# Attention and mixture kernel on Trainium2: reciprocals of all batches spread by TensorE, loads moved to slot 10 without their wait for transposes, attends at every second slot

## The chip, the cores and the metric

The kernel runs on one core of one Trainium2 chip. The metric is the time of one execution in device microseconds. Executions of one kernel mostly agreed within about 0.35%, so effects of half a per cent need several runs and a comparison on the same chip. All runs quoted here are fast (none was more than 1.5% above the fastest of its kernel).

TensorE appears in the profile as PE (matmuls) and PEld (weight loads), VectorE as DVE, ScalarE as ACT, GpSimd as POOL. SP is SyncE; its work here is to issue DMAs, and SPq is its queue.

## The reference, cut to what matters

```python
def _attn_ref(q, k, v):                      # 8 batches, 8 heads, 576 tokens, head size 64
    ...                                      # phi(x): relu(x) times cos and sin weights, 128 features
    kv  = einsum('bhsf,bhsd->bhfd', phi(k), v)
    z   = sum(phi(k), axis=2)
    num = einsum('bhsf,bhfd->bhsd', phi(q), kv)
    den = einsum('bhsf,bhf->bhs', phi(q), z)[..., None] + 1e-06
    return num / den

def _moe_ref(x, w_gate, w1, w2):             # x: 4608 tokens x 512; 8 experts, inner size 1024
    P = exp(x @ w_gate - max)                # then 8 rounds of row and column normalisation
    for e in range(8):
        out += P[:, e:e+1] * (relu(x @ w1[e]) @ w2[e])
```

## The kernel before: the parts that matter

The first fifth of the run interleaves two things on TensorE: the feed-forward of expert 0, in blocks of 512 tokens, and the attention of the batches to come. A block `j` has 16 slots; each slot is four or so 512-wide matmuls of expert 0, followed by the pieces of attention work listed for that slot. In block `j`, the batch `b = j + 1` gets its denominators and its attends, batch `b + 1` is prepared (relu, weights, transposition of q), and batch `b + 2` is loaded. The trace shows ACT taking its instructions in the order in which they are written: it stood for 6.31 us, until 110.99 us, before a k tile that was not loaded yet, while PE waited (5.08 us, until 112.21) for ACT's next instruction. The text reads the other engines in the same way, which is an assumption.

```python
def load(b, half, names="qkv", held_back=False):        # issued on POOL
    for name in names:
        x = ld.tile([P, 2, C, D], F16, name=f"{name}_ld")
        ...
        i = nc.gpsimd.dma_start(out=..., in_=...)
        if held_back:
            after(ve.last, i)        # wait for the last DVE operation written so far
            after(turned[0], i)      # wait for the last transpose written so far

def prep_q(b, hk):                   # four times per batch; q_p has 3 buffers
    ...                              # DVE: relu, then q_p = q * weights
    turned[0] = nc.sync.dma_start(out=qTs[b, hk], in_=q_p..., transpose=True)   # on SP

def denominators(b):
    ...                              # PE: 24 matmuls of zsel with qTs[b, 0..3], written h by h
    ve.reciprocal(out=den[:], in_=den[:])
    if b >= 3:                       # spread over the 64 features of a head by DMA
        r = dram.tile([96, C3 * HP], FP32, name="r")
        nc.sync.dma_start(out=r[:], in_=den[:])
        for hk in range(HK):
            for hh in range(2):      # 8 reads that repeat a row over 64 partitions
                nc.sync.dma_start(out=rb[hh * HP : (hh + 1) * HP, :]..., in_=r[:]...)
        return
    ...                              # b < 3: hi and hl = den as two fp16 parts (DVE)

def attend(b, hk):
    if not by_dma:                   # b < 3: 3 matmuls with a 0/1 matrix spread hl over features
        te.matmul(out=rb_ps[i]..., lhsT=spread..., rhs=hls[b][:])
        se.copy(out=rb[...], in_=rb_ps[i]...)          # ACT, 384 and 192 wide
    ...                              # PE: num_ps = kv x qT;  DVE: xT = num_ps * rb
```

Names that come up in the profiles: `zsel` holds the sums of k, and the zsel matmuls with transposed q make the denominators; `kv_sb` is k times v, copied out of PSUM by ACT; `hT` is the hidden layer of expert 0 after its relu, copied out of `h_ps` by ACT; `xT` is what attention hands to the experts.

The two `rb_ps`, the two `num_ps`, the sums and the denominators all come from one pool of four PSUM banks (`small_ps`). The schedule, for blocks 2 to 6 (`at(block, slot, ...)`):

```python
at(j, 5 if j <= 2 else 4, denominators, b)
at(j, 8 + 2 * hk if j == 1 else 12 + hk, attend, b, hk)          # hk = 0..3
prep_q of batch b+1 at slots 5, 7, 8, 9; prep_kv at 6, 8, 10, 12; prep_k at 4, 6, 9, 11
at(j, 10, sums, b + 1, 0)
at(j, 13 + 2 * half, load, b + 2, half, "qkv", True)             # blocks 1 to 5
```

Block 1 prepares later than the others: its four `prep_q` of batch 3 stand at slots 7, 10 and 13 and at slot 0 of block 2.

Of the kernel before, what the change touches and what calls it, by code (L numbers as in the profile page):

```python
# [10 lines left out]
FP32 = mybir.dt.float32  # L11
# [14 lines left out]
def kernel(  # L26
# [10 lines left out]
    nc = tc.nc  # L37
    P = nc.NUM_PARTITIONS
# [4 lines left out]
    HP = P // 2  # L43
# [137 lines left out]
    with ExitStack() as p1:  # L181
# [10 lines left out]


        loaded = {}
        turned = [None]
        sources = {"q": q, "k": k, "v": v}

        def load(b, half, names="qkv", held_back=False):
            for name in names:
                x = ld.tile([P, 2, C, D], F16, name=f"{name}_ld")  # L200
                view = sources[name][b].rearrange("(hk hh) (p c) d -> (hh p) hk (c d)", hh=2, c=C)
                i = nc.gpsimd.dma_start(
                    out=x[:].rearrange("p hk c d -> p hk (c d)"),
                    in_=view[:, 2 * half : 2 * half + 2],
                )
                if held_back:

                    after(ve.last, i)
                    after(turned[0], i)
                for i in range(2):  # L210
                    loaded[name, b, 2 * half + i] = x[:, i]

# [88 lines left out]
        ve.tensor_copy(out=wg[:], in_=wg_ld[:])  # L301


        kps, qps, qTs, kvs, hls, rbs = {}, {}, {}, {}, {}, {}

        lent = acc_lo[:, G_LO - 4 : G_LO, :].rearrange("p g d -> p (g d)").bitcast(F16)
        VA = C * (D + 2)
# [18 lines left out]
        def prep_q(b, hk):  # L326

            q16 = loaded.pop(("q", b, hk))
            by_dma = b >= 2
            if by_dma:  # L330
                ve.tensor_scalar(
                    out=q16, in0=q16, scalar1=0.0, scalar2=None, op0=ALU.max
                )
            q_p = qp_pool.tile([P, C, 2, D], F16, name="q_p")
            ve.tensor_tensor(
                out=q_p[:], in0=q16.unsqueeze(2).to_broadcast([P, C, 2, D]),
                in1=cs, op=ALU.mult,
            )
            if by_dma:
                qTs[b, hk] = q_pTs[(b * HK + hk) % len(q_pTs)]  # L340
                turned[0] = nc.sync.dma_start(
                    out=qTs[b, hk], in_=q_p[:].rearrange("p c a d -> p (c a d)"),
                    transpose=True,
                )
            else:
                qps[b, hk] = q_p
# [72 lines left out]
        def denominators(b):  # L419

            zsel = kvs[b][1]
            den_ps = ps_s.tile([P, 512], FP32, name="small_ps")
            for h in range(H):
                hk, hh = h // 2, h % 2
                for j in range(3):
                    te.matmul(
                        out=den_ps[32 * j : 32 * j + 32, 0 : C3 * HP],
                        lhsT=zsel[:, h, :],
                        rhs=qTs[b, hk][:, j * C3 : (j + 1) * C3, hh * HP : (hh + 1) * HP],
                        start=(h == 0),  # L430
                        stop=(h == H - 1),
                    )
            den = kv_pool.tile([96, C3 * HP], FP32, name="den")
            ve.tensor_scalar(
                out=den[:], in0=den_ps[0:96, 0 : C3 * HP], scalar1=1e-6 / XS, scalar2=None,
                op0=ALU.add,
            )
            ve.reciprocal(out=den[:], in_=den[:])
            if b >= 3:

                r = dram.tile([96, C3 * HP], FP32, name="r")
                nc.sync.dma_start(out=r[:], in_=den[:])
                for hk in range(HK):
                    rb = rb_pool.tile([P, C * HP], FP32, name="rb")
                    for hh in range(2):
                        h = 2 * hk + hh
                        nc.sync.dma_start(  # L447
                            out=rb[hh * HP : (hh + 1) * HP, :].rearrange(
                                "p (j s) -> p j s", j=3
                            ),  # L450
                            in_=r[:].rearrange("(j r) s -> r j s", r=32)[h : h + 1].to_broadcast(
                                [HP, 3, C3 * HP]
                            ),
                        )
                    rbs[b, hk] = rb
                return

            hi = kv_pool.tile([96, C3 * HP], F16, name="hi")
            ve.tensor_copy(out=hi[:], in_=den[:])
            hl = kv_pool.tile([96, C3 * HP], F16, name="hl")  # L460
            ve.scalar_tensor_tensor(
                out=hl[:], in0=hi[:], scalar=lo[0:96], in1=den[:], op0=ALU.mult, op1=ALU.add
            )
            hls[b] = hl

        def attend(b, hk):

            parts = ((0, 2 * C3), (2 * C3, C))
            rb = rbs.pop((b, hk), None)
            rb_ps = [ps_s.tile([P, 512], FP32, name="small_ps") for _ in parts if rb is None]  # L470
            by_dma = rb is not None
            if not by_dma:
                rb = rb_pool.tile([P, C * HP], FP32, name="rb")
            for i, (c0, c1) in enumerate(parts):
                if by_dma:
                    break
                for j in range(c0 // C3, c1 // C3):
                    te.matmul(
                        out=rb_ps[i][:, (j * C3 - c0) * HP : ((j + 1) * C3 - c0) * HP],
                        lhsT=spread[0:96, j, hk].rearrange("p hh d -> p (hh d)"),  # L480
                        rhs=hls[b][:],
                        start=True,
                        stop=True,
                    )
                se.copy(out=rb[:, c0 * HP : c1 * HP], in_=rb_ps[i][:, 0 : (c1 - c0) * HP])
            num_ps = [ps_s.tile([P, 512], FP32, name="small_ps") for _ in parts]
            for i, (c0, c1) in enumerate(parts):
                for hh in range(2):
                    te.matmul(
                        out=num_ps[i][hh * HP : (hh + 1) * HP, 0 : (c1 - c0) * HP],  # L490
                        lhsT=kvs[b][0][:, hk, hh, :],
                        rhs=qTs[b, hk][:, c0:c1, hh * HP : (hh + 1) * HP],
                        start=True,
                        stop=True,
                    )
                ve.tensor_tensor(
                    out=xT[:, hk, b * S + c0 * HP : b * S + c1 * HP],
                    in0=num_ps[i][:, 0 : (c1 - c0) * HP],
                    in1=rb[:, c0 * HP : c1 * HP],
                    op=ALU.mult,  # L500
                )
# [89 lines left out]
        for j in range(B):  # L591
            b = j + 1
            if j == 0:

                at(0, 4, lambda: begun.append(sums_begun(1, 0)))
                at(0, 5, lambda: sums_made(1, 0, begun[2]))
                at(0, 6, lambda: begun.append(sums_begun(1, 1)))
                at(0, 7, prep_q, 1, 0)
                at(0, 7, prep_q, 1, 1)
                for hk in range(HK):  # L600
                    for i in range(3):
                        at(0, 7 + hk, turn, 1, hk, i)
                    if hk == 0:
                        at(0, 7, lambda: sums_made(1, 1, begun[3]))
                    if hk < 2:
                        at(0, 7 + hk, prep_q, 1, hk + 2)
                at(0, 10, denominators, 1)
                at(0, 11, gates, 0)
                for hk in range(HK):
                    at(0, min(13 + hk, 15), attend, 1, hk)  # L610
            elif b < B:
                if j <= 2:
                    at(j, 0, prep_q, b, 3)
                    at(j, 1, prep_kv, b, 3)
                    at(j, 1, sums, b, 0)
                    at(j, 3, sums, b, 1)
                    for i, (hk, k_) in enumerate(turns[2:]):
                        at(j, i // 2, turn, b, hk, k_, k_ != 1)
                else:
                    at(j, 0, sums, b, 1)  # L620
                    for i, (hk, k_) in enumerate(turns[8:]):
                        at(j, i, turn, b, hk, k_, k_ != 1)
                at(j, 5 if j <= 2 else 4, denominators, b)
                for hk in range(HK):
                    at(j, 8 + 2 * hk if j == 1 else 12 + hk, attend, b, hk)
            if j:
                at(j, 6, gates, j)
            if j <= 1:
# [15 lines left out]
                at(j, 10, sums, b + 1, 0)  # L644
            if 1 <= j and b + 2 < B:
                for half in range(2):
                    at(j, 13 + 2 * half, load, b + 2, half, "qkv", True)
        y_pss = {}
        for j in range(B - 1):
            if j:  # L650
# [521 lines left out]
```

## Time and profile before

| | before |
|---|---|
| time, median of the runs taken beside the change | 1014.13 us |
| PE busy | 972.6 us of a span of 1010.5 |
| blocks 2 to 6, from the timeline of PE | 24.7, 26.7, 24.6, 24.8, 18.5 us |
| PE waits for ACT in those blocks | 14.6 us, 4 times |

The page of the profiled execution opens with busy time by engine. Its second part cuts the span into 40 slices of 25 us, with the busy share and the granted TensorE clock in tenths. Its fourth part is the chain of work that ended last, followed back from the end of the run: how much of the span was spent on whom.

```profile
PE 972.6 (96%) x7786; PEld 675.3 (67%) x7786; DVE 808.5 (80%) x1828; ACT 552.5 (55%) x1220; POOL 60.3 (6%) x82
...
PEclk8999899999999999999999999999999999999999
DMA  9949999563100431134002331043013410104535
...
PE 83%; DMA 9%; DVE 3%; ACT 1%; issue 1%; SPq 1%; POOL 1%; POOLq 0%; DVEq 0%; ACTq 0%
```

PE looks full. But the chain holds 9% of DMA, and the slices with a busy DMA are the first eight, about 200 us. That is where the change works. From about 195 us on nothing differs between the two kernels.

The next view is the list of waits between 50 and 200 us: who waited for whom, microseconds in total, times, longest.

```profile
POOL q_ld L202 <- DMA q_pT<-q_p: 43.2, 2, 22.2
...
POOL q_ld L202 <- DMA acc_hi<-q_p: 21.3, 1, 21.3
...
ACT k_ld L109 <- DMA k_ld<-in_k_dram: 19.4, 4, 6.3
...
PE h_ps L109 <- ACT hT L109: 14.6, 4, 5.1
```

Read upwards, these lines are one chain. PE waits for a PSUM buffer that ACT has not emptied (hT, 14.6 us). ACT has not, because it stands before a k tile whose load is late (19.4 us). POOL issued that load late, because it waited for transposes (43.2 and 21.3 us; q_pT, acc_lo and acc_hi are all places where transposed q is kept). The timeline of SP's queue in block 3 shows why the transposes were late. Columns: start, duration, instruction, count.

```profile
106.62 0.33 SPq L442 DMA_DIRECT2D r<-den  x1
109.09 2.38 SPq L341 DMA_TRANSPOSE q_pT<-q_p  x1
113.37 6.20 SPq L447 DMA_DIRECT2D rb<-r  x8
119.83 3.09 SPq L341 DMA_TRANSPOSE q_pT<-q_p  x1
123.03 2.38 SPq L341 DMA_TRANSPOSE acc_lo<-q_p  x1
125.52 1.30 SPq L341 DMA_TRANSPOSE acc_hi<-q_p  x1
```

The eight rb reads wait for the r write to land (6.68 us after its issue, at 113.30) and then take 6.2 us of issue. Three transposes stand behind them. The next load waits for the last transpose, issued at 125.52, and was issued at 129.38. The following block's k tile is then late again: a ring. The load and ACT's wait for its k tile, from the timelines of POOL and ACT:

```profile
129.38 0.72 POOL L202 DMA_DIRECT2D q_ld<-in_q_dram  x1 [21.29 <-DMA acc_hi<-q_p]
```

```profile
135.69 0.68 ACT L109 ACTIVATE k_ld<-k_ld 128x576 f16<-128x576 f16 x1 [4.32 <-DMA k_ld<-in_k_dram]
```

The loads of block 1 were issued at 77.30, before there was any rb read (the first at 88.60); the last that POOL had waited for was DVE (acc_lo).

The timeline of PE shows what a gap costs (blocks 2 and 3; the bracket is the idle time before the group and what ended it).

```profile
80.51 0.51 PE L109 MATMUL small_ps<-q_pT,zsel 128*32 128x192 f16 x12
...
85.53 1.04 PE L109 MATMUL h_ps<-xT,w1e 128*128 128x512 f16 x4 [2.83 <-ACT hT L109]
86.39 4.44 PE L109 MATMUL y_ps<-w2e,hT 128*128 128x512 f16 x12
...
112.21 1.87 PE L109 MATMUL h_ps<-xT,w1e 128*128 128x512 f16 x4 [5.08 <-ACT hT L109]
```

Four 512-wide matmuls take 1.04 us at a granted clock of 1.00 (85.5 to 86.4 us) and 1.87 after the gap of 5.08 us, at 0.50 (110.3 to 117.1 us). The twelve behind the first gap take 4.44 us; the clock was 0.50 there from 86.4 to 89.8 us. So each of these gaps was paid for twice: once as idle time, once as matmuls at half clock behind it.

### The profile page before, as it was taken

The page shows a single profiled execution, that of the slowest core. Times are in us where ns is not written, and L with a number is a line of the kernel's source. Part 1 is how long each engine was busy: PE and PEld are TensorE (multiplying, and loading weights), DVE is VectorE, ACT ScalarE, POOL GpSimd, SP SyncE. Part 2 cuts the span into 40 slices and gives each one's busy share as a digit, 9 for nine tenths or more (in the row PEclk, how much of TensorE's full clock was granted, in tenths as well). Part 3 has the DMA queues.
Part 4 walks back from the last instruction along what each step waited for, and adds up shares of the span by engine and source line. Part 5 has one row for each costly group of instructions (what it writes and reads, how often), then busy time and mean ns, then how long its engine had stood idle before and what let it go on. Part 6 is the DMA issues. An engine that isn't in the chain of part 4 may idle for free.

```text
span 1010.5 us, 20082 instructions
## 1 busy us (share of the span) xinstructions
PE 972.6 (96%) x7786; PEld 675.3 (67%) x7786; DVE 808.5 (80%) x1828; ACT 552.5 (55%) x1220; POOL 60.3 (6%) x82
## 2 busy tenths in 40 slices
PE   7998788998999999999999999999999999999997
PEld 6444333445777777777777777777777777777775
DVE  5876555488898888898889888889789888988886
ACT  5764343446777655555555555555555555555551
POOL 6301111001000000000000000000000000000001
PEclk8999899999999999999999999999999999999999
DMA  9949999563100431134002331043013410104535
GB/s 167 204 76 176 156 173 172 103 129 66 38 34 24 90 66 33 40 66 87 27 25 58 61 70 38 25 89 66 24 49 66 78 36 25 48 25 104 135 85 126
DMA packets 89216, 79.81 MB, mean 79 GB/s; under 512 B 33984, under 2 KB 81056, under 8 KB 89120
## 3 DMA queue, kind: packets, MB, share of 16 engines
q1 hardware_dynamic: 61648, 47.33, 20.2%
q0 software_dynamic: 27232, 30.94, 19.6%
q8 instruction: 61, 1.00, 0.4%
q10 hardware_dynamic: 240, 0.26, 0.1%
q14 instruction: 35, 0.29, 0.1%
HBM read 89.01 MB, written 13.34 MB: 101 GB/s over the span
## 4 chain that ended last, share of the span: by engine, by line
PE 83%; DMA 9%; DVE 3%; ACT 1%; issue 1%; SPq 1%; POOL 1%; POOLq 0%; DVEq 0%; ACTq 0%
PE rows_ps L109 33%; PE h_ps L109 25%; PE copied_ps L109 11%; PE p_ps L109 11%; DMA rb<-r 2%; DMA q_pT<-q_p 2%; PE small_ps L109 2%; PE y_ps L109 2%; DMA k_ld<-in_k_dram 1%; DMA v_ld<-in_v_dram 1%; DMA q_ld<-in_q_dram 1%; SPq L447 1%; DMA r<-den 1%; DVE xT L109 1%; DVE den L109 1%
## 5 line engine op out<-in xcount | busy, mean ns | idle before, releaser
L845 DVE SCALAR_TENSOR_TENSOR acc_lo<-rows_ps,P_tok,acc_lo 128x512 f32<-128x512 f32 (+1 forms) x322 | 203.5, 641 | 74.8 <-PE rows_ps L109 74.8
L109 PEld LDWEIGHTS <-H 128*128 128x128 f16 x2080 | 203.0, 98 | 83.1 <-issue 1.2
L109 PEld LDWEIGHTS <-w1e 128*128 128x128 f16 x1632 | 156.7, 98 | 82.9 <-issue 23.2
L781 ACT CAST u<-h_ps 128x384 f16<-128x384 f32 x288 | 137.8, 478 | 131.2 <-PE h_ps L109 131.2
L775 DVE CUSTOM_DVE_ANT_0 H<-p_ps,u 128x384 f16<-128x384 f32 x329 | 181.4, 551 | 6.6 <-PE p_ps L109 6.5
L109 PEld LDWEIGHTS <-hs 128*128 128x128 f16 x1500 | 146.5, 98 | 56.4 <-issue 0.3
L109 PE MATMUL h_ps<-xT,w1e 128*128 128x384 f16 (+1 forms) x616 | 152.5, 354 | 17.8 <-ACT hT L109 14.6
L109 PE MATMUL h_ps<-S,w1e 128*128 128x384 f16 x672 | 164.1, 326 | 1.1 <-ACT u L109 0.9
L109 PE MATMUL p_ps<-xT,T 128*128 128x384 f16 x672 | 164.1, 326 | 0.1
L109 PE MATMUL rows_ps<-V,H 128*128 128x256 f16 x1000 | 150.0, 273 | 0.7 <-DVE acc_hi L845 0.7
L109 PE MATMUL rows_ps<-w2e,hs 128*128 128x256 f16 x1000 | 150.0, 273 | 0.0
L813 ACT ACTIVATE H<-h_ps 128x384 f16<-128x384 f32 x144 | 70.7, 491 | 95.0 <-PE h_ps L109 95.0
L109 PEld LDWEIGHTS <-T 128*128 128x128 f16 x1008 | 98.1, 98 | 29.5 <-issue 3.2
L109 PE MATMUL rows_ps<-w2e,H 128*128 128x256 f16 (+1 forms) x568 | 91.2, 285 | 0.0
L794 ACT COPY copied_ps<-h_ps 128x384 f32<-128x384 f32 x144 | 67.5, 468 | 35.4 <-PE h_ps L109 35.4
L109 PE MATMUL h_ps<-S,T 128*128 128x384 f16 x336 | 81.8, 325 | 0.4 <-ACT copied_ps L109 0.3
L109 PE MATMUL copied_ps<-xT,w1e 128*128 128x384 f16 x336 | 82.1, 326 | 0.0
L804 ACT ACTIVATE H<-copied_ps 128x384 f16<-128x384 f32 x144 | 70.9, 492 | 20.3 <-PE copied_ps L109 20.3
L109 PE MATMUL copied_ps<-w2e,H 128*128 128x256 f16 x504 | 75.5, 272 | 0.0
L109 PE MATMUL rows_ps<-V,hs 128*128 128x256 f16 x500 | 75.0, 272 | 0.0
L845 DVE SCALAR_TENSOR_TENSOR acc_lo<-copied_ps,P_tok,acc_lo 128x256 f32<-128x256 f32 x126 | 60.2, 478 | 0.6 <-PE copied_ps L109 0.2
L109 PE MATMUL y_ps<-w2e,hT 128*128 128x512 f16 x224 | 60.0, 410 | 0.6 <-ACT acc_lo L109 0.6
(135 smaller groups left out, 914.1 us busy)
## 6 DMA issues: line engine op xcount, KB each, us to landing
S<-x_saved SPq DMA_DIRECT2D x108, 192.0 KB, 2.4
out_dram<-acc_lo SPq DMA_DIRECT2D x62, 128.0 KB, 2.4
w1e<-in_moe_w_dram POOLq DMA_DIRECT2D x7, 1024.0 KB, 8.9
w2e<-in_moe_w_dram POOLq DMA_DIRECT2D x7, 1024.0 KB, 9.7
rb<-r SPq DMA_DIRECT2D x40, 144.0 KB, 5.7
k_ld<-in_k_dram POOLq DMA_DIRECT2D x16, 288.0 KB, 9.3
v_ld<-in_v_dram POOLq DMA_DIRECT2D x16, 288.0 KB, 10.3
q_ld<-in_q_dram POOLq DMA_DIRECT2D x16, 288.0 KB, 8.7
```

Of the source, the lines that this page charges most:

```text
L109: i = getattr(self.engine, name)(*args, **kwargs)
L447: nc.sync.dma_start(out=rb[hh * HP : (hh + 1) * HP, :].rearrange("p (j s) -> p j s", j=3), in_=r[:].rearrange("(j r) s -> r j s", r=32)[h ...
L775: latest = ve._custom_dve(TENSOR_ADD_SAT, out=out, in0=ps[:, 0:TU], in1=t[:], s0=FP32_MAX, s1=0.0)
L781: se.copy(out=t[:], in_=ps[:, 0:TU])
L794: se.copy(out=Y[:, 0:TU], in_=X[:, 0:TU])
L804: se.activation(out=h11, in_=Y[:, 0:TU], func=AF.Relu)
L813: se.activation(out=h12, in_=X[:, 0:TU], func=AF.Relu)
L845: ve.scalar_tensor_tensor(out=a, in0=rows, scalar=P_tok[:, g, self.e : self.e + 1], in1=a, op0=ALU.mult, op1=ALU.add,)
```

## The change

Its intent is to cut that ring. Three parts: (1) the reciprocals of all batches are spread over features by matmuls, as batches 0 to 2 already were, so the r write and the rb reads leave SP's queue; (2) loads are issued from slot 10 on and no longer wait for a transpose; (3) attends of blocks 2 to 6 sit at slots 8, 10, 12, 14, as those of block 1 already did.

```diff
                 if held_back:
                     after(ve.last, i)
-                    after(turned[0], i)
...
             ve.reciprocal(out=den[:], in_=den[:])
-            if b >= 3:
-                r = dram.tile([96, C3 * HP], FP32, name="r")
-                nc.sync.dma_start(out=r[:], in_=den[:])
-                ...                                     # the 8 rb reads
-                return
             hi = kv_pool.tile([96, C3 * HP], F16, name="hi")
...
-            rb = rbs.pop((b, hk), None)
-            rb_ps = [... for _ in parts if rb is None]
-            by_dma = rb is not None
-            if not by_dma:
-                rb = rb_pool.tile([P, C * HP], FP32, name="rb")
+            rb_ps = [ps_s.tile([P, 512], FP32, name="small_ps") for _ in parts]
+            rb = rb_pool.tile([P, C * HP], FP32, name="rb")
...
-                    at(j, 8 + 2 * hk if j == 1 else 12 + hk, attend, b, hk)
+                    at(j, 8 + 2 * hk, attend, b, hk)
...
-                    at(j, 13 + 2 * half, load, b + 2, half, "qkv", True)
+                    at(j, 10 + half, load, b + 2, half, "qkv", True)
```

More of the change, by code (lines that the diff above doesn't have):

```diff
@@ L194 @@
         loaded = {}
-        turned = [None]
         sources = {"q": q, "k": k, "v": v}
@@ L301 @@
         ve.tensor_copy(out=wg[:], in_=wg_ld[:])
-        kps, qps, qTs, kvs, hls, rbs = {}, {}, {}, {}, {}, {}
+        kps, qps, qTs, kvs, hls = {}, {}, {}, {}, {}
         lent = acc_lo[:, G_LO - 4 : G_LO, :].rearrange("p g d -> p (g d)").bitcast(F16)
@@ L340, in prep_q @@
                 qTs[b, hk] = q_pTs[(b * HK + hk) % len(q_pTs)]
-                turned[0] = nc.sync.dma_start(
+                nc.sync.dma_start(
                     out=qTs[b, hk], in_=q_p[:].rearrange("p c a d -> p (c a d)"),
@@ L438, in denominators @@
             ve.reciprocal(out=den[:], in_=den[:])
-            if b >= 3:
-                r = dram.tile([96, C3 * HP], FP32, name="r")
-                nc.sync.dma_start(out=r[:], in_=den[:])
-                for hk in range(HK):
-                    rb = rb_pool.tile([P, C * HP], FP32, name="rb")
-                    for hh in range(2):
-                        h = 2 * hk + hh
-                        nc.sync.dma_start(
-                            out=rb[hh * HP : (hh + 1) * HP, :].rearrange(
-                                "p (j s) -> p j s", j=3
-                            ),
-                            in_=r[:].rearrange("(j r) s -> r j s", r=32)[h : h + 1].to_broadcast(
-                                [HP, 3, C3 * HP]
-                            ),
-                        )
-                    rbs[b, hk] = rb
-                return
             hi = kv_pool.tile([96, C3 * HP], F16, name="hi")
@@ L468, in attend @@
             parts = ((0, 2 * C3), (2 * C3, C))
-            rb = rbs.pop((b, hk), None)
-            rb_ps = [ps_s.tile([P, 512], FP32, name="small_ps") for _ in parts if rb is None]
-            by_dma = rb is not None
-            if not by_dma:
-                rb = rb_pool.tile([P, C * HP], FP32, name="rb")
+            rb_ps = [ps_s.tile([P, 512], FP32, name="small_ps") for _ in parts]
+            rb = rb_pool.tile([P, C * HP], FP32, name="rb")
             for i, (c0, c1) in enumerate(parts):
-                if by_dma:
-                    break
                 for j in range(c0 // C3, c1 // C3):
```

## The prediction

> **What bounds the kernel now.** The page gives PE 972.6 us busy of 1010.5 (96%). From about 195 us on PE hardly waits and the change touches nothing there. It acts on five blocks (each a pass of expert 0 over 512 tokens) between 73.7 and 193 us. The timeline of PE gives their lengths: 24.7, 26.7, 24.6, 24.8, 18.5 us. The last has no preparation and no loads; it shows what PE needs.
>
> The difference is a ring of waits, read from the waits view and the timelines: PE's h_ps waits for ACT's hT (2.8, 5.1, 3.2, 3.5 us, once in each of the first four blocks); ACT sits before it on a k_ld relu that waits for the k load (19.4 us, 4 times); POOL issued that load late, because it waited for transposes (43.2 and 21.3 us); the transposes stood on SP's queue behind the r write (6.7 us to landing under load) and eight rb reads (0.61 us each to issue, 5.7 to land). After each gap PE runs slowly: twelve 512-wide y_ps matmuls take 4.3 to 4.4 us instead of 2.7. [...] Gaps and slow restarts cost 4.5, 7.6, 4.9, 5.1 = 22 us.
>
> **Removed:** 5 r writes, 40 rb reads (6.4 us of the 16 DMA engines per block by their packets), SP's queueing. The ring is cut: loads can start at slot 10, and their k half lands about 7 us after issue, before slot 4 of the next block. The 22 us should mostly go.
>
> **Added:** 20 times three spread matmuls, 0.34 us of PE pitch each (block 1 has them), 6.8 us on PE, wholly critical. ACT: 40 copies of about 0.48/0.32 us; DVE: hi and hl, 0.7 us per block; both have room on average.
>
> **New waits.** (a) Preparation and attends now share slots 8 to 14 with the sums of slot 10 on four PSUM banks. Adding DVE durations in order (q 1.0, kv 1.0, reciprocal chain 2.4, attend 0.8) puts DVE about 2 us behind there; the third attend waits for the sums' banks: estimate 1 us of PE in four blocks. (b) Block 1's loads move from 77.3 to about 70 us, onto the last two transposes of batch 3 (issued 73.5 and 76.4). Under loads a transpose took 8.4 us to land instead of 3.2. Denominators of batch 3 (PE at 80.5 us) may wait to 84 or 85, with a slow restart: about 4 us in block 2. In later blocks the load still waits for the last DVE operation written before it (the sums' zsel), so it follows the transposes.
>
> **Sum:** -22 + 6.8 + 4 (a) + 4 (b) = about -8. Predicted 1005 us, 996 to 1015 for 8 in 10. Even without new waits the gain is 15 us (1.5%), so over 2% faster has chance 0.03; slower by over 2% 0.02; within 2% 0.95.
>
> **What would show it.** Right: no rb reads from DRAM; ACT's wait for k_ld near 0 from 98 us on; h_ps no longer waiting 3 to 5 us for hT; blocks of 21 to 23 us, the last about 20; fewer half-clock entries. (a) right: small_ps matmuls waiting for ACT kv_sb or DVE xT after slot 10. (b) right: one PE gap of 3 to 6 us at about 80 us, before the zsel matmuls, released by a transpose.
>
> **What would make it wrong.** Transposes starving under the earlier loads in every block (to 1020); loads 11.3 + transposes 8.3 us of DMA per block of about 21 is nearly full. Or DVE keeping up and transposes sharing fairly: 998.

The 22 us are the four gaps and the slow matmuls behind them, read from the timeline of PE.

## The result, and the profile after

The change took 1007.0 us in the median (1005.13 to 1007.32, 4 runs), beside 1014.13 (1013.33 to 1015.21, 4 runs). The ratio is 0.9925, 95% interval 0.9908 to 0.9942: 0.75% faster. A ratio here is the mean time of one kernel's fast runs over that of the other's of the same rounds, so not quite the ratio of the quoted medians. A second set of runs of the change, taken later beside an experiment, gave 1005.43 us and 0.992.

The page of the change, the same parts as before:

```profile
PE 974.6 (97%) x7846; PEld 681.4 (68%) x7846; DVE 810.0 (81%) x1838; ACT 566.3 (56%) x1260; POOL 60.3 (6%) x82
...
PEclk8997999999999999999999999999999999999999
DMA  9947885353101331034013321043113410104535
...
PE 91%; DVE 4%; DMA 2%; ACT 1%; issue 1%; POOL 1%; DVEq 0%; POOLq 0%; ACTq 0%; SPq 0%
```

DMA has nearly left the chain (2% against 9%). One slice of the stretch that the change touches still has a low clock (0.7), the fourth (about 75 to 100 us). The waits of the change between 74 and 190 us, those of PE:

```profile
PE small_ps L109 <- DMA acc_lo<-q_p: 6.4, 1, 6.4
PE small_ps L109 <- ACT kv_sb L109: 4.2, 4, 1.2
PE small_ps L109 <- ACT rb L109: 0.8, 4, 0.3
PE small_ps L109 <- DMA acc_hi<-q_p: 0.5, 1, 0.5
```

The wait of PE for hT is gone, and so is every wait of ACT for a k load. In their place stand one wait of 6.4 us for a transpose and four small ones for kv_sb. The timeline of PE shows where (blocks 2 and 3):

```profile
81.85 0.51 PE L109 MATMUL small_ps<-q_pT,zsel 128*32 128x192 f16 x12
88.73 0.51 PE L109 MATMUL small_ps<-acc_lo,zsel 128*32 128x192 f16 x6 [6.38 <-DMA acc_lo<-q_p]
89.72 0.51 PE L109 MATMUL small_ps<-acc_hi,zsel 128*32 128x192 f16 x6 [0.47 <-DMA acc_hi<-q_p]
90.16 1.89 PE L109 MATMUL h_ps<-xT,w1e 128*128 128x512 f16 x4
...
124.14 0.44 PE L109 MATMUL small_ps<-q_pT,kv_sb 128*64 128x384 f16 x4 [1.21 <-ACT kv_sb L109]
```

The first zsel matmuls of batch 3 run; those for the third and fourth pair of heads must wait for their transposed q. The restart is again at half clock (1.89 us for four; granted clock 0.50 from 85.6 to 95.8 us). SP's queue in the same blocks:

```profile
74.86 3.24 SPq L339 DMA_TRANSPOSE acc_lo<-q_p  x1
78.27 6.15 SPq L339 DMA_TRANSPOSE acc_hi<-q_p  x1
...
120.95 1.28 SPq L339 DMA_TRANSPOSE acc_lo<-q_p  x1
122.34 1.31 SPq L339 DMA_TRANSPOSE acc_hi<-q_p  x1
```

At 120.95 a transpose takes 1.3 us to issue; at 74.86 and 78.27 it takes 3.2 and 6.2. The timeline of POOL says what else was there: block 1's six loads begin at 71.60, block 3's at 124.22, just behind the transposes.

```profile
71.60 0.71 POOL L201 DMA_DIRECT2D q_ld<-in_q_dram  x1 [30.31 <-DVE q_p L109]
...
124.22 0.72 POOL L201 DMA_DIRECT2D q_ld<-in_q_dram  x1 [16.90 <-DVE zsel L109]
```

How long such a transpose is under way is in the view of DMA issues between 72 and 82 us (KB are left out for transposes; the last number is the median from issue to landing in us). First the kernel before, whose loads came later (77.30), then the change:

```profile
acc_lo<-q_p SPq DMA_TRANSPOSE x1, 3.2
acc_hi<-q_p SPq DMA_TRANSPOSE x1, 3.2
```

```profile
acc_lo<-q_p SPq DMA_TRANSPOSE x1, 13.8
acc_hi<-q_p SPq DMA_TRANSPOSE x1, 11.4
```

To compare all runs, one number per block is useful: the time from the first zsel matmul of one batch to the first of the next, worked out from the starts of these matmuls in each trace. The period of batch 3 covers the wait in block 2.

| kernel | batch 3 | batch 4 | batch 5 | batch 6 | sum, us |
|---|---|---|---|---|---|
| before | 23.46 | 26.70 | 24.49 | 25.29 | 99.9 |
| the change | 29.85 | 21.33 | 21.34 | 21.33 | 93.9 |

Three periods shrank by 12.5 us in all (76.48 to 64.00), and one grew by 6.4. The net is 6.1 us, while the span fell by 4.9 (1010.5 to 1005.6). From the first zsel matmul of the last batch to the end nothing changed: 830.1 us before, 829.9 after. The first zsel matmul of batch 3 came 1.3 us later in this execution of the change (81.85 against 80.51), because PE ran at half clock from 54.9 to 58.3 us (granted clock 0.50 there, 0.79 over 54 to 62 us), before anything that the change touches. No gap of PE near it is longer than 0.88 us; several short waits stand in a row there. The other profile of the change has slow matmuls there too (six 512-wide ones in 3.02 us). That of the kernel before has no such stretch (granted clock 1.00 over 54 to 62 us), and neither have those of some kernels with the same code up to there (parts 1 and 3 of the change: 1.62 us for the same six); it is not an effect of the change.

### The profile page after: what moved, and what is told of

It reads as the page before. It is cut to its first block, busy times and chain, and to the rows that moved or that the text cites. A ratio compares the mean times of both kernels' runs of the same rounds, so it can differ in the third digit from the quotient of the medians.

```text
span 1005.6 us, 20219 instructions
## 1 busy us (share of the span) xinstructions
PE 974.6 (97%) x7846; PEld 681.4 (68%) x7846; DVE 810.0 (81%) x1838; ACT 566.3 (56%) x1260; POOL 60.3 (6%) x82
## 4 chain that ended last, share of the span: by engine, by line
PE 91%; DVE 4%; DMA 2%; ACT 1%; issue 1%; POOL 1%; DVEq 0%; POOLq 0%; ACTq 0%; SPq 0%
PE rows_ps L109 33%; PE h_ps L109 27%; PE copied_ps L109 11%; PE p_ps L109 11%; PE y_ps L109 5%; PE small_ps L109 4%; DMA acc_hi<-q_p 1%; DVE xT L109 1%; DMA k_ld<-in_k_dram 1%; DVE k_p L109 1%; DVE den L109 0%; DVE acc_lo L109 0%; ACT rb L109 0%; DVE acc_hi L819 0%; POOL hs_last L834 0%
## 5 line engine op out<-in xcount | busy, mean ns | idle before, releaser
L819 DVE SCALAR_TENSOR_TENSOR acc_hi<-rows_ps,P_tok,acc_hi 128x512 f32<-128x512 f32 (+1 forms) x56 | 41.3, 737 | 20.1 <-PE rows_ps L109 19.3
```

Source lines behind the costliest of these rows:

```text
L819: ve.scalar_tensor_tensor(out=a, in0=rows, scalar=P_tok[:, g, self.e : self.e + 1], in1=a, op0=ALU.mult, op1=ALU.add,)
```

## The experiments

Ten more runs were made, nine of other kernels and one of the change again, all with correct results. They ran on three chips. Every ratio is to the kernel before, run in the same rounds on the same chip, so compare ratios before medians. Edits are shown against the change, unless said otherwise; the lines that only record the last transpose in `turned` are left out.

### 1. The three parts, taken apart

The change without part 2 (loads back at slots 13 and 15, behind the transposes):

```diff
+                    after(turned[0], i)
-                    at(j, 10 + half, load, b + 2, half, "qkv", True)
+                    at(j, 13 + 2 * half, load, b + 2, half, "qkv", True)
```

> The change without its second part: reciprocals by TensorE and attends every second slot stay, loads go back to slots 13 and 15 behind the transposes. Theory (the spreading alone unblocks SP's queue and so the transposes; dropping the wait in block 1 costs): no gap before the zsel matmuls of block 2, instead about 2.8 us of h_ps waiting for hT there as before; later blocks 21.3 to 22.5 us, the k load at most 2 us late; 1001 to 1005 us, so 2 to 6 us faster than the change. Rival (dropping the wait is where the gain comes from): later blocks stay at 24 to 25 us, total about 1014 us.

Part 2 alone, on the kernel before:

```diff
-                    after(turned[0], i)
-                    at(j, 13 + 2 * half, load, b + 2, half, "qkv", True)
+                    at(j, 10 + half, load, b + 2, half, "qkv", True)
```

> The kernel before with only the loads moved: slots 10 and 11, no wait for transposes; rb still by DMA, attends at 12 to 15. Theory: ACT's wait for the k load goes, but SP's queue keeps the rb reads ahead of transposes and DMA has 26 us of packets per block instead of 20, so blocks stay at 22.5 us or more, and block 2 gets the gap for transposes too; 1007 to 1016 us. Rival (early loads alone make the gain): 1005 to 1007 us, blocks of about 21 us.

The change without part 3 (attends back at slots 12 to 15 in blocks 2 to 6):

```diff
-                    at(j, 8 + 2 * hk, attend, b, hk)
+                    at(j, 8 + 2 * hk if j == 1 else 12 + hk, attend, b, hk)
```

> The change without its third part: attends of blocks 2 to 6 back at slots 12 to 15, one per slot, reciprocals still spread by TensorE, loads as in the change. Theory (four attends in a row, each of four banks, outrun DVE and ACT, and the last product of xT comes too late for the next block): waits of small_ps for DVE xT or ACT rb and of h_ps for xT add to 2 us or more per block, against 1.2 us now; blocks of 22 to 23 us; 1009 to 1015 us. Rival (slots 8 to 14 are themselves the trouble, since preparation of the next batch sits there): the wait for kv_sb goes and blocks shorten to about 20.5 us; 1002 to 1005 us.

Part 1 alone (both of the undoings above):

> The first part of the change alone: reciprocals of all batches spread by TensorE; attends back at slots 12 to 15 and loads back at 13 and 15 behind the transposes. Theory (this part brings the gain, the attends add about 1.3 us per block, the moved loads cost about 6 us in block 2 only): no gap before zsel, one gap of about 3.5 us for hT in block 2, blocks of about 22.6 us, total 1004 to 1007 us. Rival (the parts help only together): total 1011 us or more.

And the change itself again, beside part 1 alone:

> The change itself once more, beside the run of its first part. Nothing new: 1005 to 1008 us, the gap before the zsel matmuls of block 2 at 6 to 7 us, blocks 3 to 5 at 21.3 us.

| kernel | median us | ratio, 95% interval | batch 3 | batch 4 | batch 5 | batch 6 |
|---|---|---|---|---|---|---|
| part 1 alone | 1007.75 | 0.9946 (0.9929 to 0.9962) | 27.30 | 22.64 | 22.64 | 22.63 |
| part 2 alone | 1037.16 | 1.0208 (1.0165 to 1.0251) | 28.94 | 34.87 | 30.11 | 34.08 |
| parts 1 and 2 | 1011.70 | 0.9995 (0.9979 to 1.001) | 30.13 | 22.63 | 22.63 | 22.63 |
| parts 1 and 3 | 1000.77 | 0.9873 (0.9856 to 0.989) | 24.98 | 21.33 | 21.33 | 21.32 |
| the change (1, 2, 3) | 1007.00 | 0.9925 (0.9908 to 0.9942) | 29.85 | 21.33 | 21.34 | 21.33 |
| the change again | 1005.43 | 0.992 (0.9901 to 0.9939) | 29.39 | 21.33 | 21.33 | 21.33 |

Part 2 loses in all three settings. With parts 1 and 3 present it adds 4.9 us to the period of batch 3 (24.98 to 29.85) and nothing to the later ones, equal within 0.01 us. Even with the wait and the late slots the later loads are in time for PE (ACT's waits for k loads add to 5.6 us, of which one in block 2 has 4.8). I put that down to part 1, which takes the reads out of SP's queue. My theory in the expectation of the first experiment held in this (there was no gap before the zsel matmuls of block 2, but one of 3.65 us for hT, foretold as 2.8; the time, 1000.77 us, was just under its range); its rival, that dropping the wait brings the gain, fell.

On the kernel before, part 2 costs 2.1%. I had expected at most 1016 us, and missed. Its waits between 48 and 205 us show what I had underrated:

```profile
PE small_ps L109 <- DMA q_pT<-q_p: 24.8, 6, 8.3
PE small_ps L109 <- DMA acc_lo<-q_p: 14.8, 2, 8.2
```

There the rb reads still hold the transposes back on SP until the early loads have begun (in one block the reads are issued from 128.43 to 133.95 us, the next transpose and the first load at 134.05, and the last two transposes take 6.55 and 7.31 us to issue). So the collision that the change has once happens in every block, and PE waits 39.6 us for transposed q. The wait and the late slot that part 2 removes together were thus not needless in the kernel before: they kept loads off the transposes. Which of the two did it there, no run separates.

Part 3 is worth 1.3 us per period with either loads (22.63 to 21.33). With attends one slot apart, the timeline of PE (part 1 alone, one block) has a row of small waits, where the change has one wait of 1.21 us and one of 0.17:

```profile
115.42 0.46 PE L109 MATMUL small_ps<-acc_lo,k_p 64*128 64x65 f16 x18 [0.49 <-DVE acc_lo L109]
118.90 0.44 PE L109 MATMUL small_ps<-q_pT,kv_sb 128*64 128x384 f16 x4 [0.94 <-ACT kv_sb L109]
120.50 0.47 PE L109 MATMUL small_ps<-hl,acc_hi 96*128 96x192 f16 x3 [0.20 <-ACT rb L109]
126.01 0.38 PE L109 MATMUL h_ps<-xT,w1e 128*128 128x512 f16 x1 [0.28 <-DVE xT L109]
```

These add to 1.9 us, against 1.4 in the change: 0.5 of the 1.3 us. The rest is in PE's busy time, 20.6 us of the period against 19.9 for the same matmuls; why they run less densely was not tested. For the change without part 3 I had expected waits of 2 us or more per block; its trace has the same four, 1.9 us in all, and its time landed in the range foretold. Part 1 alone landed at 1007.75, just above its range of 1004 to 1007.

### 2. Is it block 1's loads that delay the transposes?

Keep the change, but issue the loads of block 1 at slots 2 and 3, so that they are over by the time the last transposes are issued. Their buffers are free there.

```diff
-                    at(j, 10 + half, load, b + 2, half, "qkv", True)
+                    at(j, 2 + half if j == 1 else 10 + half, load, b + 2, half, "qkv", True)
```

> The change with block 1's loads at slots 2 and 3 instead of 10 and 11, so that they are over when the last transposes of batch 3 are issued. Theory (those loads starve those transposes): the 6.4 us gap before the zsel matmuls in block 2 falls under 0.5 us, the slow matmuls behind it go as well, total 997 to 1000 us, 7 to 9 us faster than the change. Rival (the transposes are late for another reason, as SP's queue, the q_p buffers or DVE): the gap stays over 3 us and the total over 1003 us.

It took 997.85 us, ratio 0.9842 (0.9823 to 0.9861). The zsel matmuls of batch 3, in its timeline of PE:

```profile
80.89 0.51 PE L109 MATMUL small_ps<-q_pT,zsel 128*32 128x192 f16 x12
81.22 0.34 PE L109 MATMUL small_ps<-acc_lo,zsel 128*32 128x192 f16 x6
81.39 0.34 PE L109 MATMUL small_ps<-acc_hi,zsel 128*32 128x192 f16 x6
```

No wait is left, and the period of batch 3 is 21.33 us like the others: 8.5 us less than in the change, of which 6.9 were the gap; the rest is put down to the slow restart (granted clock 0.50 from 85.6 to 95.8 us in the change). SP's queue, the q_p buffers and DVE are the same in both kernels, so the rival fell. An earlier transpose of batch 3 took 4.9 us to land there, against 3.2 for the last two, but nobody needs it before 80 us.

Does the wait alone protect? The wait put back, the slot left at 10:

```diff
+                    after(turned[0], i)
```

> The change with the wait for the transpose last issued put back, but loads still written at slots 10 and 11. Theory: in block 1 the load waits for the second transpose (issued 71.4) only and starts at about 75 to 76 us, still on top of the last two, so the gap in block 2 shrinks only in part, to 2 to 5 us; later blocks 21.3 us as now; 1001 to 1006 us. Rival (the wait alone, at whatever slot, protects): no gap before zsel, about 1001 us.

It took 1007.76 us, ratio 0.9955 (0.9937 to 0.9973), and both of my readings missed: the gap was neither gone nor smaller. The load waited for the second transpose and was issued at 73.71 us, not at 75; the third transpose slipped through in 5.9 us to landing, and the fourth, 14.0 us, met the whole of the loads. Its entry in the chain of waits, and the matmul behind it in the timeline of PE:

```profile
76.27 13.97 DMA acc_hi<-q_p
```

```profile
90.28 0.51 PE L109 MATMUL small_ps<-acc_hi,zsel 128*32 128x192 f16 x6 [9.19 <-DMA acc_hi<-q_p]
```

Here the wait protected only what was issued before the load. What counted in these runs is that no transpose needed soon is issued while loads are in flight: 3.2 us to landing in the early loads' run, 11.4 to 14.0 among the whole of them.

### 3. The four PSUM banks

The sums of the next batch, moved behind the attends:

```diff
-                at(j, 10, sums, b + 1, 0)
+                at(j, 15, sums, b + 1, 0)
```

> The change with the first sums of the next batch at slot 15 instead of 10, behind all attends. Theory (the third attend waits for the banks of these sums until DVE has made zsel): the wait of 1.2 us for ACT kv_sb in blocks 3, 4, 5 and 0.6 us in block 2 goes, blocks of about 20.1 us, total 1002 to 1003.5 us. Rival (the four banks are short whatever the order, or DVE is the limit): the wait moves to another matmul, blocks stay over 21 us, total 1006 to 1008 us. The gap of 6.4 us in block 2 stays in both.

It took 1002.86 us, ratio 0.9895 (0.9878 to 0.9913). The wait for kv_sb is gone; a wait of 0.54 us for ACT rb remains at the third attend, and the periods of batches 4 to 6 fall from 21.33 to 20.25, 20.23 and 20.25 us. So the place of the sums was the cost, not the number of banks alone. The edit moves the request for banks and the work of DVE and ACT that empties them together; which of the two counts was not separated.

### 4. What the added matmuls cost

Each spread matmul of batches 3 to 7 issued twice, with the same values:

```diff
-                for j in range(c0 // C3, c1 // C3):
+                for j in [j for _ in range(1 + (b >= 3)) for j in range(c0 // C3, c1 // C3)]:
```

> The change with each spread matmul of batches 3 to 7 issued twice, same values. Theory A (as predicted blind: their 0.34 us per attend are wholly critical on PE): 6 to 7 us slower than the change, 1013 to 1014 us. Theory B (in blocks 2 to 5 the chain of DVE before the third attend sets the pace, so up to 1.2 us of PE work ahead of it is hidden in the wait for kv_sb): the wait shrinks to 0.2 us, blocks 3 to 5 grow by only 0.4 us, block 6 by 1.4; 2 to 4 us slower, 1009 to 1011 us.

It took 1008.24 us (theory B had said 1009 to 1011), ratio 0.996 (0.9944 to 0.9976): 3.5 us more than the change by the ratios (0.996 less 0.9925, of 1012), 1.6 by the profiled spans (1007.2 against 1005.6). Periods 4 to 6 grew by 0.25 us only, although 12 matmuls were added to each. A second set of three is cheaper than the first: six take 0.59 us from their start to the next group, where three took 0.34. So about 1.0 us was added to each block. The wait for kv_sb shrank by half (0.6 us less) and the wait of 0.17 us is gone, which leaves the 0.25:

```profile
115.74 0.66 PE L109 MATMUL small_ps<-hl,acc_hi 96*128 96x192 f16 x6
116.33 0.44 PE L109 MATMUL small_ps<-q_pT,kv_sb 128*64 128x384 f16 x4
...
123.45 0.44 PE L109 MATMUL small_ps<-q_pT,kv_sb 128*64 128x384 f16 x4 [0.62 <-ACT kv_sb L109]
```

So three quarters of what was added in blocks 3 to 5 was hidden. In block 6, where PE has no wait, nothing was: from the zsel matmuls to the next block it took 14.56 us instead of 13.56. Spread matmuls are thus not "wholly critical" in blocks 3 to 5, as I had written; PE waits there for zsel on DVE and the copy on ACT behind it (in block 3 of the change PE 1.21 us for ACT kv_sb, and ACT before that 3.82 us for DVE zsel). What the first set costs was not measured by taking it away; that it too is mostly hidden is inferred.

### 5. Both repairs together

```diff
-                at(j, 10, sums, b + 1, 0)
+                at(j, 15, sums, b + 1, 0)
-                    at(j, 10 + half, load, b + 2, half, "qkv", True)
+                    at(j, 2 + half if j == 1 else 10 + half, load, b + 2, half, "qkv", True)
```

> The change with both repairs: block 1's loads at slots 2 and 3, and the sums of the next batch at slot 15. Theory (the two waits lie in different places, so their gains add): no gap over 1 us before the zsel matmuls, no wait for ACT kv_sb, blocks of about 20.3 us from block 2 on, total 992 to 995 us. Rival (with the gap closed the loads or transposes of the shorter blocks collide next): a new gap of 2 us or more before zsel or for hT, total over 996 us.

It took 993.21 us (990.43 to 993.78, 4 runs), ratio 0.9807 (0.9787 to 0.9826), the fastest kernel. The periods are 19.80, 20.25, 20.23, 20.25 us: 80.5 in all, against 93.9 in the change and 99.9 before. The only waits of PE left between 74 and 190 us are these:

```profile
PE small_ps L109 <- ACT rb L109: 2.2, 4, 0.5
PE small_ps L109 <- DVE xT L109: 0.3, 1, 0.3
```

## Why the prediction was right, and where it was off

- **Time.** 1005 us predicted, 1007.0 and 1005.43 measured, inside 996 to 1015 and within 2%. That the sum came out has some luck in it: (b) was put at 4 us and cost 8.5, while the spread matmuls and (a), put at 6.8 and 4 and added in full, overlap. And part 3 was counted as a cost alone, in (a); the runs show that it is worth 1.3 us per period once the reciprocals are spread by matmuls (22.63 to 21.33).
- **The ring, and that part 1 cuts it.** Right. Part 1 alone takes away the wait for the k load in all blocks but block 2, where block 1's late load remains. Of the four gaps that the prediction counts to the ring, that one was none of it. Whether the freed queue of SP or the 6.4 us of DMA time per block that left with the reads does it, no run separates; the traces show both (1632 packets of 768 bytes per block, 6.3 to 6.5 us in blocks 2 to 5 of the kernel before and none in the change). In block 3 of the kernel before, DVE had the second q_p ready at 113.89, but its transpose was issued at 119.83, 5.9 us later, behind the reads, and then took 6.55 us to land; in part 1 alone the four transposes of that block are issued between 112.35 and 119.14 us with nothing else on SP's queue, and in the change, whose queue holds no reads either, those of that block landed after 3.2 to 3.3 us.
- **"The 22 us should mostly go."** Right for the blocks where it was read: periods 4 to 6 lost 12.5 us net of the added work, and the blocks are 21.3 us, as foretold (21 to 23). The gain that I put down to early loads was not theirs: with parts 1 and 3 present the later blocks are the same with late loads.
- **Spread matmuls, "6.8 us on PE, wholly critical".** The size is right (0.34 us of pitch each), the second half is not: doubling them added about 1.0 us of PE work per block and cost 0.25 us per period in blocks 3 to 5. Block 6, foretold at about 20 us, came to 18.8.
- **(a), the banks.** Right in place and size (banks and the DVE work behind them moved together, as said above): 1 us in four blocks foretold, 1.21 in three and 0.6 in one measured, and moving the sums took it away. But (a) and the spread matmuls share the same time and should not have been added in full.
- **(b), block 1's loads on batch 3's transposes.** The mechanism was foretold, with place and releaser; its size was half of the truth. I took 8.4 us to landing from blocks of the kernel before where a transpose met the tail of the loads (8.40 and 8.50 us, issued at 160.30 and 135.43), and added one. The last two met the whole of them and took 13.8 and 11.4 us. Predicted cost about 4 us, shown by the early loads of experiment 2 to be 8.5.
- **Later blocks, where loads follow the transposes through the wait for zsel.** Right: the last transpose of block 3 was issued at 122.34, the first load at 124.22.
- **Half clock.** Foretold and seen: four stretches between 75 and 175 us became one. In the kernel before the granted clock was 0.50 from 86.4 to 89.8, 110.3 to 117.1, 137.6 to 141.0 and 161.5 to 164.9 us, and 1.00 between them; the gaps of PE that ended at 85.5, 112.2, 136.9 and 161.8 were of 2.83, 5.08, 3.19 and 3.53 us. In the change it was 0.50 from 85.6 to 95.8 us, in and behind the gap that began at 82.3, and 1.00 from there to 190. After the fourth gap of the kernel before the twelve y_ps matmuls took 3.46 us, not 4.3 to 4.4 as the prediction has it for each.

## What to carry to other kernels

When a wait is removed, ask which transfers it kept apart: a wait, or a late place in the order, that looks like a needless delay of a load may be what keeps a transfer that is needed soon (here a DMA transpose) clear of a burst of loads (3.2 us to landing became 11.4 to 14.0). Place bulk loads where nothing that is needed soon is issued while they are in flight, and check each block by itself, since the first block after a change of pace can collide where the steady ones do not (here a period of 29.85 us beside three of 21.33). And take a change of several parts apart: here one part of three gave back about two fifths of what the other two had gained (ratio 0.9873 without it, 0.9925 with it). Undoing it was worth 0.5% and re-placing it 0.8%, where the change itself was worth 0.75%.

## What the traces show of transposes beside loads, and of slow stretches

- A transpose of 128x1152 fp16 values landed after 3.2 to 3.3 us with no load packet moving (the change, 117 to 124 us), and after 11.4 to 14.0 us when six loads of 288 KB were in flight (the change and the run with the wait put back).
- The same number of packets took very different time. In the trace of the change, where both kinds move, between 80 and 85 us there were, as the profile counts packets, 675 of loads and 670 of transposes. A data packet of a load has 1152 bytes there and one of a transpose 256, and the transposes had 0.29 of the engines' time and the loads 0.91 (the sum is over 1, so packets overlap in the record). At the start it was otherwise: from 74.86 us, when the first late transpose was issued, to 78.86 the profile has 552 packets of loads and 32 of 4 bytes on the transposes' queue, none with data. The cause of that stays open.
- The shortest gap with a slow stretch behind it in the kernel before was of 2.83 us (the last 512-wide matmul had ended 3.2 us before the next began; sixteen small ones ran just before the gap): the granted clock was 0.57 from 86 to 90 us, and twelve matmuls took 4.44 us instead of about 2.7. The three waits of 1.21 us in the change had none behind them (granted clock 1.00 from 95.9 to 190 us). What happens in between was not examined, and the stretch at 54.9 us of the change, with no gap over 0.88 us near it, is not explained.
